# Batch 0 of a routed attention kernel: transposes of pairs 4 to 6 placed up to three steps sooner, alpha's column moved from step 39 to step 10

## Chip, cores and metric

The kernel runs on one core of one Trainium2 chip. The metric is the device time of one execution in microseconds (us), lower is better. A profile is one execution taken by the hardware profiler; its span is about 1.8 us shorter than the timed value of the same execution. All timed runs quoted as ratios are fast (granted TensorE clock 0.99 to 1.00); of the kernel before, one run of 320.57 us at a clock of 0.95 was left out as slow.

## The reference, cut to what matters

Four batches, eight heads, 768 positions, head size 64. Each query and key is assigned to the nearest of 16 centroids, and a query attends only to keys of its own cluster. The result goes through a hidden layer of 2048 columns with a "snake" activation.

```python
mask = q_assign[:, :, :, None] == k_assign[:, :, None, :]
scores = np.where(mask, scale * (q @ k.T), -1e9);  attn = softmax(scores)
x = (attn @ v) reshaped to [3072, 512]
h = x @ w_in;  g = h + sin(alpha * h)**2 / (alpha + 1e-9);  out = g @ w_out
```

## The kernel before

Heads are done in pairs. Batch 0 is a loop of 48 steps, 12 for each of its pairs 0 to 3. In step i TensorE makes scores for one block of keys, ScalarE takes their exp, and TensorE multiplies an earlier step's exps with V ("PV"). In between TensorE prepares later pairs: it transposes q and k ("T units", four to a pair, three 128x128 transposes each) into one of three PSUM banks, VectorE evicts them (copies them out, so that the bank is free again), and GpSimd casts the result. For each pair VectorE also makes a one-hot of the cluster ("one-hot chain": `asT`, `amax`, the is_equal `ohd`, `ohT`). `at(i, f)` only fixes the place of f in each engine's program order; nothing waits for a clock.

```python
banks = [M1, M2, M0]                       # taken in turn by bank()
def prep_T(m, g, bk=None, eng="dve"):      # one T unit
    ...
    for jj in range(NJ2):                  # 3 transposes on TensorE
        nc.tensor.transpose(out=bk[:, P*jj : P*jj+P], in_=src[:, h, P*jj : P*jj+P], identity=ident_f)
    nc.vector.tensor_scalar_mul(out=s["T32"][:, g, :], in0=bk[:, 0:HS], scalar1=1.0 / QDIV)   # the line shown as L150
def pair_steps(m, make, asn, cast):
    for g, i in make:      at(i, lambda g=g: prep_T(m, g))
    for h in range(2):     at(cast[h], lambda h=h: prep_cast(m, h))        # GpSimd
    ...
    at(asn,     lambda: (prep_asn(m), prep_hot(m, 0)))                    # asT
    at(asn + 1, lambda: (prep_hot(m, 1), prep_hot(m, 2)))                 # amax, is_equal
    at(asn + 2, lambda: (prep_hot(m, 3), prep_move(m)))                   # ohT and its DMA
def pv(i):
    ...                                    # 6 matmuls into OB
    if kt == NJ - 1:                       # last step of a head: free OB
        nc.vector.reciprocal(out=rec, in_=o3[:, :, D : D + 1])
        nc.vector.tensor_tensor(out=s["xs"][:, :, h, :], in0=o3[:, :, 0:D], in1=rec..., op=ALU.mult)
def alpha():
    bk = bank()
    nc.tensor.transpose(out=bk[:, 0:NF], in_=a_sb, identity=ident_f[0:NF, 0:NF])
    nc.vector.tensor_copy(out=alpha_col, in_=bk[:, 0:NF])                    # L639
    nc.vector.tensor_scalar_add(out=ralpha, in0=alpha_col, scalar1=1e-9)     # L640
    nc.vector.reciprocal(out=ralpha, in_=ralpha)                             # L641
...
for r in range(ASTEPS):                    # 48 steps
    scores(i); expo(i)
    ahead = b == 0 and r % NJ == 1         # in these steps the plan stands before PV
    if ahead: (plan of step i)
    for d in due.get(r, []): pv(base + d)
    if not ahead: (plan of step i)
```

The softmax here doesn't subtract the row's maximum and nothing guards it: scores larger than these inputs give would overflow.

Of the kernel before, what the change touches and what calls it, by code (L numbers as in the profile page):

```python
# [22 lines left out]
def kernel(  # L23
# [78 lines left out]
    def bank():  # L102
        while True:
            i = turn[0] % 3
            turn[0] += 1
            if i not in held:
                return banks[i]
# [27 lines left out]
    def prep_T(m, g, bk=None, eng="dve"):  # L135

        s = st[m]
        if "T32" not in s:
            s["T32"] = trp.tile([P, 4, HS], F32, tag="T32", name="T32")
        h, t = divmod(g, 2)  # L140
        src = s["q32" if t == 0 else "k32"]
        bk = bank() if bk is None else bk
        for jj in range(NJ2):
            nc.tensor.transpose(  # L144
                out=bk[:, P * jj : P * jj + P],
                in_=src[:, h, P * jj : P * jj + P],
                identity=ident_f,
            )
        if eng == "dve":
            nc.vector.tensor_scalar_mul(  # L150
                out=s["T32"][:, g, :], in0=bk[:, 0:HS], scalar1=1.0 / QDIV
            )
        else:
            nc.scalar.activation(
                out=s["T32"][:, g, :], in_=bk[:, 0:HS], func=ACTF.Copy, scale=1.0 / QDIV
            )
# [203 lines left out]
    def x_T(m, bk=None):  # L360
        b, hp = pair_of[m]
        xs = st[m]["xs"]
        xt_ps = (bank() if bk is None else bk).bitcast(BF16)[:, 0:S]
        for j in range(NJ):
            nc.tensor.transpose(
                out=xt_ps.rearrange("c (i j a) -> c j i a", i=4, j=NJ)[:, j],
                in_=xs[:, j, :, :],
                identity=ident_b,
            )
        nc.vector.tensor_copy(out=xT[:, hp, :], in_=xt_ps)  # L370
        st[m].clear()
# [3 lines left out]
    def x_D(m):  # L375
        hp = pair_of[m][1]
        if hp == 0:
            xq[0] = xqp.tile([P, 2 * S], BF16, tag="xq", name="xq")
        nc.vector.transpose(  # L379
            out=xq[0][:, S * hp : S * hp + S],  # L380
            in_=st[m]["xs"].rearrange("p j h (e d) -> p (h e) j d", e=2),
        )
        st[m].clear()
# [178 lines left out]
    def at(i, fn):  # L562
        plan.setdefault(i, []).append(fn)
# [10 lines left out]
    def pair_steps(m, make, asn, cast):  # L574
        for g, i in make:
            at(i, lambda g=g: prep_T(m, g))
        for h in range(2):
            at(cast[h], lambda h=h: prep_cast(m, h))
        if asn is None:
            return  # L580
        at(asn, lambda: (prep_asn(m), prep_hot(m, 0)))
        at(asn + 1, lambda: (prep_hot(m, 1), prep_hot(m, 2)))
        at(asn + 2, lambda: (prep_hot(m, 3), prep_move(m)))
# [9 lines left out]
    for m, make, asn, cast in (  # L593
        (1, (), 1, (0, 0)),
        (2, ((0, 4), (2, 5), (1, 6), (3, 7)), 8, (7, 8)),
        (3, ((0, 12), (1, 14), (2, 16), (3, 17)), 20, (14, 18)),
        (4, ((0, 19), (1, 23), (2, 24), (3, 26)), 32, (24, 28)),
        (5, ((0, 28), (1, 30), (2, 31), (3, 34)), 38, (31, 35)),
        (6, ((0, 35), (1, 36), (2, 37), (3, 40)), None, (37, 41)),
    ):  # L600
        pair_steps(m, make, asn, cast)
    for g, i in enumerate((41, 42, 43)):
        at(i, lambda g=g: prep_T(NHP + 3, g))
    for h in range(2):
        at(ASTEPS + 4 + 2 * h, lambda h=h: prep_cast(NHP + 3, h))
# [5 lines left out]
    for b in range(1, B):  # L611
        for n in range(NHP):
            m = NHP * b + 3 + n
# [10 lines left out]
    for m in range(NP):  # L624
        if m % NHP != NHP - 1:
            if m < NHP:
                at((18, 29, 44)[m], lambda m=m: x_T(m))
            elif m % NHP == 2:
                at(STEPS * (m + 1) + 4, lambda m=m: x_T(m))
            else:  # L630
                at(STEPS * (m + 1) + 5, lambda m=m: x_D(m))
# [8 lines left out]
        nc.vector.tensor_scalar_add(out=ralpha, in0=alpha_col, scalar1=1e-9)  # L640
        nc.vector.reciprocal(out=ralpha, in_=ralpha)  # L641

    at(39, alpha)
    def load_w_in(n):
        nc.gpsimd.dma_start(
            out=w_in_bf[:, :, 512 * n : 512 * n + 512],
            in_=moe_w_in[:, 512 * n : 512 * n + 512].rearrange("(kk p) f -> p kk f", p=P),
        )
# [24 lines left out]
    for b in range(B):  # L673
        base = ASTEPS * b
        fill = Fill(b - 1) if b else None
        for r in range(ASTEPS):
            i = base + r
# [105 lines left out]
```

## Time and profile before

| kernel before | |
|---|---|
| time, median of the first 3 runs | 313.48 us (312.94 to 313.51) |
| span of the profiled execution | 312.8 us |
| TensorE busy | 302.7 us |
| batch 0's exps: first starts, last ends | 11.91 us, 53.75 us |

From the page of the kernel before: its span, the busy time of the engines (PE is TensorE, PEld its weight loads, DVE is VectorE, ACT ScalarE, POOL GpSimd), and the shares of the chain that ended last.

```profile
span 312.8 us, 7228 instructions
...
PE 302.7 (97%) x2750; PEld 179.9 (58%) x2750; DVE 208.9 (67%) x367; ACT 239.5 (77%) x324; POOL 139.0 (44%) x222
...
PE 86%; DVE 5%; ACT 4%; DMA 2%; issue 1%; SPq 1%; ACTq 0%; DVEq 0%
```

TensorE is the bounding engine over the whole span. A busy share of 97% says where to look, not how much is left: the Trainium skill, "Perfetto Trace Analysis", section "Identifying the Most-Contended Engine", warns that matmul busy time is no good measure of the distance to the limit, because matmuls are pipelined. So the useful question is where TensorE waits. Busy time by stretches (microseconds from the span's start, then busy time of each engine with its instruction count) shows one such place at the end of batch 0's loop.

```profile
core 0: us, PE busy (x) PEld busy (x) DVE busy (x) ACT busy (x) POOL busy (x), PEclk, DMA share, GB/s
36.00:48.00 12.00, 12.00 (x157) 8.51 (x154) 10.82 (x22) 10.57 (x14) 11.32 (x14) 1.00 1.06 243
48.00:53.30 5.30, 4.10 (x59) 2.87 (x57) 3.55 (x9) 4.05 (x6) 3.68 (x5) 1.00 0.59 101
```

In the second stretch TensorE is busy for 4.10 of 5.30 us. VectorE's order of work before and in that stretch (start, duration, engine, line, operation, result and sources) tells why.

```profile
44.69 0.58 DVE L243 STREAM_TRANSPOSE asT<-M 128x384 f32<-128x384 f32 x1
45.31 0.55 DVE L246 TENSOR_REDUCE amax<-asT 128x24 f32<-128x384 f32 x1
45.90 1.10 DVE L254 TENSOR_TENSOR ohd<-asT,amax 128x384 bf16<-128x384 f32 x1
46.92 0.16 DVE L639 COPY alpha_col<-M 128x16 f32<-128x16 f32 x1
47.12 0.60 DVE L640 TENSOR_SCALAR ralpha<-alpha_col 128x16 f32<-128x16 f32 x1
47.75 0.25 DVE L641 RECIPROCAL ralpha<-ralpha 128x16 f32<-128x16 f32 x1
48.13 0.58 DVE L280 STREAM_TRANSPOSE ohT<-ohd 128x384 bf16<-128x384 bf16 x1
48.63 1.91 DVE L150 TENSOR_SCALAR T<-M 128x384 f32<-128x384 f32 x4
50.46 0.18 DVE L352 RECIPROCAL rec<-OB 128x6 f32<-128x6 f32 x1
50.68 0.56 DVE L353 TENSOR_TENSOR xs<-OB,rec 128x384 bf16<-128x384 f32 x1
```

The is_equal (L254) of pair 5 takes 1.10 us. Alpha's three operations follow (L639 to L641), and the add of 16 columns alone takes 0.60 us. Only then comes the one-hot's transpose at 48.13, and four evictions (L150) stand behind it, then rec and xs. GpSimd was casting meanwhile.

```profile
45.77 1.92 POOL L186 CAST QK<-T 64x768 bf16<-64x768 f32 x2
```

Casts occupy GpSimd from 45.77 to 47.69. TensorE's own timeline shows what it waited for (in brackets: idle time just before, and who ended it).

```profile
49.20 0.55 PE L144 MATMUL M<-ident_f,q 128*128 128x128 f32 x3 [0.57 <-DVE T L150]
...
51.29 0.52 PE L341 MATMUL OB<-VX,pT 128*128 128x65 bf16 x12 [0.36 <-DVE xs L353]
```

Step 43's transposes had to wait for a bank (the weight load that goes with them had stood for 0.96 us), and PV of step 45 had to wait for xs. The chain of waits in the same stretch (start, duration, what) runs through VectorE without a break.

```profile
48.64 1.90 DVE T L150 x4
50.54 0.11 DVE rec L352
...
50.68 0.57 DVE xs L353
```

### The profile page before, as it was taken

Reading aid. Unit: us, or ns where it says so; the run is one execution under the profiler, and the core shown is the slowest. Engines: PE = TensorE matmul, PEld = TensorE weight load, DVE = VectorE, ACT = ScalarE, POOL = GpSimd, SP = SyncE. Lnnn points to the kernel's source line nnn. Section 1 sums busy time; section 2 is a strip of 40 time slices with the busy share of each in tenths; the row PEclk is TensorE's granted clock in tenths of the full one; section 3 lists DMA queues with packets and bytes.
Section 4 is the critical chain, followed back from the end, with each engine's and each line's share of the span. In section 5 each row is a group of like instructions: output and inputs, shape, how many; then the busy total and the mean of one; then the engine's idle time right before and its main releaser. Section 6 shows DMA issues by size and latency. Waiting matters only on the chain.

```text
span 312.8 us, 7228 instructions
## 1 busy us (share of the span) xinstructions
PE 302.7 (97%) x2750; PEld 179.9 (58%) x2750; DVE 208.9 (67%) x367; ACT 239.5 (77%) x324; POOL 139.0 (44%) x222
## 2 busy tenths in 40 slices
PE   8899998999999999999999999999999999999994
PEld 3466776455456656555556556555556666555443
DVE  4777796688866876677867877686935313687711
ACT  6589988787679998688679998688679999777200
POOL 5979997109506099985006079980001190000000
PEclk9999999999999999999999999999999999999999
DMA  7549996958753567991044477420011121000032
GB/s 232 146 159 292 310 232 128 196 93 285 233 135 79 106 163 171 261 347 60 0 124 113 98 171 163 114 84 2 0 67 49 37 49 39 34 0 2 0 134 69
DMA packets 28674, 38.92 MB, mean 124 GB/s; under 512 B 5072, under 2 KB 22496, under 8 KB 28640
## 3 DMA queue, kind: packets, MB, share of 16 engines
q0 software_dynamic: 10240, 21.11, 25.8%
q1 hardware_dynamic: 18160, 17.30, 20.6%
q8 instruction: 22, 0.36, 0.5%
q14 instruction: 12, 0.10, 0.1%
q10 hardware_dynamic: 240, 0.06, 0.1%
HBM read 27.30 MB, written 6.29 MB: 107 GB/s over the span
## 4 chain that ended last, share of the span: by engine, by line
PE 86%; DVE 5%; ACT 4%; DMA 2%; issue 1%; SPq 1%; ACTq 0%; DVEq 0%
PE M L394 19%; PE S L425 17%; PE S L326 12%; PE OB L341 10%; PE M L425 8%; PE S L327 6%; PE OB L394 5%; PE M L214 3%; DMA QK<-ohT 2%; PE S L394 2%; ACT pT L332 2%; PE M L144 2%; DVE gT L450 2%; ACT s_sb L438 1%; DVE T L150 1%; DVE u_sb L446 1%
## 5 line engine op out<-in xcount | busy, mean ns | idle before, releaser
L332 ACT ACTIVATE pT<-S 128x768 bf16<-128x768 f32 x192 | 143.7, 810 | 17.6 <-PE S L327 16.1
L394 PE MATMUL M<-w_out_bf,gT 128*128 128x512 bf16 (+1 forms) x288 | 90.7, 373 | 0.2
L326 PE MATMUL S<-QK 80*128 80x512 bf16 x192 | 72.9, 380 | 1.5 <-DMA QK<-ohT 1.2
L425 PEld LDWEIGHTS <-w_in_bf 128*128 128x128 bf16 x512 | 49.3, 98 | 37.9 <-issue 1.8
L341 PEld LDWEIGHTS <-pT 128*128 128x128 bf16 x1152 | 56.1, 97 | 21.4 <-issue 0.5
L425 PE MATMUL S<-xT,w_in_bf 128*128 128x512 bf16 x352 | 65.0, 326 | 0.7 <-DVE gT L450 0.6
L341 PE MATMUL OB<-VX,pT 128*128 128x65 bf16 x1152 | 61.3, 193 | 0.6 <-DVE xs L353 0.4
L438 ACT ACTIVATE s_sb<-S,alpha_col 128x768 bf16<-128x768 f32 (+2 forms) x45 | 39.3, 885 | 23.7 <-PE S L425 16.1
L394 PEld LDWEIGHTS <-gT 128*128 128x128 bf16 x400 | 39.0, 97 | 30.7 <-issue 5.4
L327 PE MATMUL S<-QK 80*128 80x256 bf16 x192 | 51.9, 270 | 0.0
L191 POOL TENSOR_SCALAR QK<-T 64x384 bf16<-64x384 f32 x64 | 34.9, 546 | 37.9 <-DMA T<-Tq 33.8
L450 DVE SCALAR_TENSOR_TENSOR gT<-u_sb,ralpha,S 128x768 bf16<-128x768 bf16 (+2 forms) x45 | 44.7, 996 | 9.7 <-ACT u_sb L443 6.8
L387 POOL DMA_DIRECT2D xT<-xq x48 | 25.8, 544 | 29.0 <-DVE xq L379 28.0
L186 POOL CAST QK<-T 64x768 bf16<-64x768 f32 x32 | 27.1, 848 | 7.7 <-DVE T L150 3.5
L425 PE MATMUL M<-xT,w_in_bf 128*128 128x512 bf16 (+1 forms) x160 | 29.9, 326 | 0.0
L352 DVE RECIPROCAL rec<-OB 128x6 f32<-128x6 f32 x32 | 6.2, 193 | 34.8 <-PE OB L341 34.8
L446 DVE TENSOR_TENSOR u_sb<-s_sb 128x768 bf16<-128x768 bf16 (+2 forms) x41 | 23.7, 580 | 7.0 <-ACT s_sb L438 7.0
L327 PEld LDWEIGHTS <-QK 80*128 80x128 bf16 x192 | 18.8, 98 | 16.1 <-issue 2.0
L203 POOL CAST VX<-v 128x768 bf16<-128x768 f32 x16 | 13.7, 859 | 28.7 <-issue 27.8
L438 ACT ACTIVATE s_sb<-M,alpha_col 128x512 bf16<-128x512 f32 (+1 forms) x40 | 20.9, 573 | 7.2 <-PE M L425 7.2
L450 DVE SCALAR_TENSOR_TENSOR gT<-u_sb,ralpha,M 128x512 bf16<-128x512 bf16 (+1 forms) x40 | 22.8, 611 | 5.4 <-ACT u_sb L443 5.0
L394 PE MATMUL OB<-w_out_bf,gT 128*128 128x512 bf16 (+1 forms) x80 | 26.2, 358 | 0.1
(83 smaller groups left out, 282.2 us busy)
## 6 DMA issues: line engine op xcount, KB each, us to landing
T<-Tq SPq DMA_DIRECT2D x64, 96.0 KB, 2.5
out_dram<-o_sb SPq DMA_DIRECT2D x23, 256.0 KB, 2.1
v<-in_v_dram POOLq DMA_DIRECT2D x14, 384.0 KB, 4.6
q<-in_q_dram POOLq DMA_DIRECT2D x13, 384.0 KB, 6.4
k<-in_k_dram POOLq DMA_DIRECT2D x13, 384.0 KB, 6.8
w_in_bf<-in_moe_w_in_dram POOLq DMA_DIRECT2D x4, 512.0 KB, 7.9
w_out_bf<-in_moe_w_out_dram POOLq DMA_DIRECT2D x4, 512.0 KB, 9.1
xT<-xq POOLq DMA_DIRECT2D x48, 24.0 KB, 2.2
```

The source lines that it names most:

```text
L186: nc.gpsimd.tensor_copy(out=QK[0:D, m % NQK, h, :, HS * par : HS * par + HS], in_=src)
L191: nc.gpsimd.tensor_scalar(out=QK[0:D, m % NQK, h, t].rearrange("c (n i a) -> c i n a", i=4, a=32)[:, 2 * par : 2 * par + 2], in0=src[:, t] ...
L326: nc.tensor.matmul(out=dst[:, 0:512], lhsT=lhsT, rhs=T[:, 0, 0:512], start=True, stop=True)
L327: nc.tensor.matmul(out=dst[:, 512:S], lhsT=lhsT, rhs=T[:, 0, 512:S], start=True, stop=True)
L332: nc.scalar.activation(out=pT, in_=area(i)[:, 0:S], func=ACTF.Exp, scale=escale)
L341: nc.tensor.matmul(out=o3[:, j, :], lhsT=pT[:, P * j : P * j + P], rhs=VX[m % NVX][:, h, jof(m // NHP, kt), :], start=(kt == 0 and j == 0) ...
L387: nc.gpsimd.dma_start(out=xT[32 * g : 32 * g + 32, 0:2, QS * i : QS * i + QS], in_=xq[0].rearrange("p (h g n) -> p h g n", h=2, g=4)[32 * ...
L394: nc.tensor.matmul(out=bk[:, lo:hi], lhsT=gT[:, f, P * mt : P * mt + P], rhs=w_out_bf[:, f, lo:hi], start=(f == 0), stop=(f == NF - 1),)
L425: nc.tensor.matmul(out=ar[lo // 512][:, 0 : hi - lo] if isinstance(ar, tuple) else ar[:, lo:hi], lhsT=lhsT, rhs=xT[:, kk, :].rearrange("c ...
L438: nc.scalar.activation(out=s_sb[:, lo:hi], in_=src, func=ACTF.Sin, scale=alpha_col[:, f : f + 1])
L446: nc.vector.tensor_tensor(out=u_sb[:, lo:hi], in0=s_sb[:, lo:hi], in1=s_sb[:, lo:hi], op=ALU.mult)
L450: nc.vector.scalar_tensor_tensor(out=gT[:, f, lo:hi], in0=u_sb[:, lo:hi], scalar=ralpha[:, f : f + 1], in1=src, op0=ALU.mult, op1=ALU.add,)
```

## The change

The intent was to take work out of VectorE's queue near the end of the loop: eleven of the twelve T units of pairs 4 to 6 come one to three steps sooner, and alpha, which is not needed before the hidden layer, goes to step 10. Three smaller moves go with it: the casts of pairs 4 to 6 come one or two steps sooner, pair 7's third T unit one step later, and pair 2's x transposes one step sooner.

```diff
-        (4, ((0, 19), (1, 23), (2, 24), (3, 26)), 32, (24, 28)),
-        (5, ((0, 28), (1, 30), (2, 31), (3, 34)), 38, (31, 35)),
-        (6, ((0, 35), (1, 36), (2, 37), (3, 40)), None, (37, 41)),
+        (4, ((0, 19), (1, 22), (2, 23), (3, 24)), 32, (23, 26)),
+        (5, ((0, 26), (1, 28), (2, 30), (3, 31)), 38, (30, 34)),
+        (6, ((0, 34), (1, 35), (2, 36), (3, 37)), None, (36, 40)),
     ...
-    for g, i in enumerate((41, 42, 43)):
+    for g, i in enumerate((41, 42, 44)):        # T units of pair 7
     ...
-                at((18, 29, 44)[m], lambda m=m: x_T(m))
+                at((18, 29, 43)[m], lambda m=m: x_T(m))
     ...
-    at(39, alpha)
+    at(10, alpha)
```

## The prediction

> **What bounds the kernel now.** TensorE: the page's engine table has it busy 302.7 of 312.8 us, and the chain that ended last is 86% TensorE. The change touches only the attention loop of batch 0 (48 steps of scores, exp and PV, about 11.4 to 53.8 us). There TensorE's queue is full, 12.00 busy of 12.00 us in the stretch 36 to 48 us, but only 4.10 of 5.30 us in 48.0 to 53.3 us (busy time by stretches). That hole is the target. The chain of waits puts VectorE on the path there: four T evictions, 48.64 to 50.54, then rec and xs to 51.25.
>
> How it arises (timeline): VectorE runs pair 5's one-hot chain from 44.69; the is_equal takes 1.10 us instead of 0.56, alpha's three operations take 46.92 to 48.00 (the add of 16 columns 0.60), and the one-hot's transpose comes only at 48.13. Four T evictions queue behind. So TensorE's transposes of step 43 wait 0.96 us for a PSUM bank (scores of step 43 start at 48.14, of step 44 at 49.77), and PV of step 45 waits about 0.5 us for xs (to 51.29).
> The two slow operations end as the GpSimd casts of 45.77 to 47.69 end. The Trainium skill, "SBUF — State Buffer", section "Who interferes with whom", says that VectorE operations with two SBUF inputs, or in two-port modes, and GpSimd exclude each other on one port pair; 1.10 against 0.56 agrees.
>
> **What changes.** No work is added or removed. Pair 4's transposes come one or two steps sooner, pairs 5 and 6 one to three, and alpha (TensorE about 0.16 us, VectorE 1.0) goes from step 39 to step 10. At step 10 TensorE waits for the one-hot DMA of step 12 anyway (idle 0.38 us in 20 to 22 us), and VectorE's next eviction starts only at 22.72, after 0.60 us of idleness; without a cast beside it alpha should take about 0.5 us. a_sb landed by 10 us.
>
> **Costing.** A step with one transpose unit takes 0.87 us (TensorE bound), one without about 0.72 (exps 0.72 apart, ScalarE bound).
> - Before step 38 one more unit is done: +0.15 to +0.35 us. GpSimd is full from 19.5 to 47.7 (13.7 of 14.0 us in 22 to 36), so its casts hardly come sooner.
> - Steps 39 and 40 lose alpha and a unit: 0.95 and 0.88 become about 0.70 and 0.76: -0.4.
> - Steps 43 to 46 lose the wait for the bank (1.63 becomes 0.85) and part of the wait for xs, perhaps 0.3 us of which stays: -0.9 in sum.
> Together the loop ends about 1.0 us sooner (0.7 to 1.4). Behind it comes the hidden layer, whose TensorE queue is nearly full to the end; its weights land before use, and batch 1's loads are paced by it. So nearly all should reach the end.
>
> **Predicted**: 312.4 us, range 311.7 to 313.2; faster by over 2%: 0.01, within 2%: 0.98, slower by over 2%: 0.01.
>
> **What would show it.** Right: no wait of transposes for T evictions in steps 41 to 44; the add under alpha well below 0.6 us; last exp of batch 0 ending about 1 us sooner (53.75 before); idle TensorE there down from 1.2 to about 0.4 us; later stages unchanged in length. The is_equal of pair 5 may stay near 1.1 us.
> Wrong: a new TensorE gap at steps 12 to 15 or 22 to 27 (VectorE now crowded by the one-hots of pairs 2 and 3), or the gain given back after 56 us.
>
> **What would make it wrong.** The one-hot chain meeting casts at other places, so that evictions pile up again; the extra unit before step 38 costing its full 0.36 us or waiting for banks; weight DMAs displaced; or run to run spread (0.6 us over three runs), which is more than half the effect.

## The result

The changed kernel took 312.38 us (median of 4 runs, 311.55 to 312.81), beside 313.26 us for the kernel before (4 runs). The ratio is 0.9969, with a 95% interval of 0.9945 to 0.9993. A ratio here is the mean time of one kernel's fast runs over that of the other's in the same rounds, so it is not quite the ratio of the medians. Two later sets of five rounds gave 0.9965 (0.9949 to 0.9981) and 0.9955 (0.9925 to 0.9985). All lie below 1.

The page after, same parts as before:

```profile
span 310.5 us, 7224 instructions
...
PE 302.7 (97%) x2750; PEld 180.0 (58%) x2750; DVE 208.6 (67%) x367; ACT 239.7 (77%) x324; POOL 139.3 (45%) x222
...
PE 87%; ACT 5%; DVE 4%; DMA 2%; issue 1%; SPq 0%; ACTq 0%; DVEq 0%
```

Busy time of every engine is unchanged, as it must be when work is only moved. The span is 2.3 us shorter, but that is not all due to the change: the last matmul ends at 307.18 us instead of 308.18, and the rest is the landing of the last store, which took 4.6 us after the last matmul in this profile of before, 4.8 us in one later profile of the changed kernel, and 3.3 us in all others, before's second one included. The stretches after:

```profile
36.00:48.00 12.00, 11.91 (x157) 8.37 (x156) 10.67 (x21) 10.74 (x15) 11.59 (x16) 1.00 1.01 238
48.00:53.30 5.30, 4.86 (x69) 3.58 (x68) 2.58 (x6) 5.02 (x7) 4.90 (x7) 1.00 0.96 167
```

TensorE's idle time in 48.0 to 53.3 us fell from 1.20 to 0.44 us. VectorE's order after:

```profile
45.07 0.58 DVE L243 STREAM_TRANSPOSE asT<-M 128x384 f32<-128x384 f32 x1
...
46.28 1.07 DVE L254 TENSOR_TENSOR ohd<-asT,amax 128x384 bf16<-128x384 f32 x1
47.39 0.58 DVE L280 STREAM_TRANSPOSE ohT<-ohd 128x384 bf16<-128x384 bf16 x1
47.89 1.01 DVE L150 TENSOR_SCALAR T<-M 128x384 f32<-128x384 f32 x2
49.00 0.56 DVE L370 COPY xT<-M 128x768 bf16<-128x768 bf16 x1
49.48 0.18 DVE L352 RECIPROCAL rec<-OB 128x6 f32<-128x6 f32 x1
49.70 0.56 DVE L353 TENSOR_TENSOR xs<-OB,rec 128x384 bf16<-128x384 f32 x1
```

Alpha is gone from it; two evictions (pair 7's first two) and the copy of pair 2's x transposes (L370, which had stood behind xs), not four evictions, stand before rec and xs; and ohT, at 47.39, comes 0.74 us sooner. The is_equal still takes 1.07 us. TensorE's timeline after:

```profile
49.31 0.49 PE L144 MATMUL M<-ident_f,q 128*128 128x128 f32 x3
...
50.30 0.52 PE L341 MATMUL OB<-VX,pT 128*128 128x65 bf16 x12 [0.17 <-DVE xs L353]
```

The transposes of pair 7's third unit, which had waited for a bank, no longer wait, and the wait for xs fell from 0.36 to 0.17 us. Alpha in its new place, step 10, on VectorE:

```profile
22.22 0.14 DVE L639 COPY alpha_col<-M 128x16 f32<-128x16 f32 x1
22.39 0.17 DVE L640 TENSOR_SCALAR ralpha<-alpha_col 128x16 f32<-128x16 f32 x1
22.60 0.25 DVE L641 RECIPROCAL ralpha<-ralpha 128x16 f32<-128x16 f32 x1
22.98 0.56 DVE L150 TENSOR_SCALAR T<-M 128x384 f32<-128x384 f32 x1
```

There it takes 0.63 us from the first start to the end of the last operation, and the add takes 0.17 us.

By intervals between the starts of exps, so that the varying start of the loop drops out (both columns from the traces):

| stretch | before | after | difference |
|---|---|---|---|
| exp 12 to exp 22 (behind alpha's new place) | 8.36 | 8.36 | 0.00 |
| exp 22 to exp 38 (one T unit more) | 13.41 | 13.53 | +0.12 |
| exp 38 to exp 43 (alpha and a unit fewer) | 4.79 | 4.40 | -0.39 |
| exp 43 to the end of exp 47 (the waits) | 5.02 | 4.04 | -0.98 |
| sum | 31.59 | 30.34 | -1.25 |

(The sum adds unrounded terms.) The loop starts 0.18 us later in the second trace and ends 0.98 us sooner; the last exp of batches 1, 2 and 3 ends 0.99, 0.98 and 1.01 us sooner. Nothing was given back.

### The profile page after: what moved, and what is told of

The parts are those of the page before. It is cut to its first block, busy times and chain, and to the rows that moved or that the text cites. A ratio compares the mean times of both kernels' runs of the same rounds, so it can differ in the third digit from the quotient of the medians.

```text
span 310.5 us, 7224 instructions
## 1 busy us (share of the span) xinstructions
PE 302.7 (97%) x2750; PEld 180.0 (58%) x2750; DVE 208.6 (67%) x367; ACT 239.7 (77%) x324; POOL 139.3 (45%) x222
## 4 chain that ended last, share of the span: by engine, by line
PE 87%; ACT 5%; DVE 4%; DMA 2%; issue 1%; SPq 0%; ACTq 0%; DVEq 0%
PE M L394 19%; PE S L425 17%; PE S L326 13%; PE OB L341 10%; PE M L425 8%; PE S L327 6%; PE OB L394 5%; PE M L214 3%; ACT pT L332 3%; PE S L394 2%; DMA QK<-ohT 2%; PE M L144 2%; DVE gT L450 2%; ACT s_sb L438 1%; DVE u_sb L446 1%; PE S L501 1%
```

## The experiments

The measure in what follows is the time from the start of exp 12 to the end of exp 47 of batch 0, read from each trace. It repeats to 0.01 us for the changed kernel (30.34, 30.34, 30.35), while whole times scatter by 0.6 us or more, so whole times cannot rank these variants. The theories:

- **A**: VectorE's queue behind pair 5's one-hot chain is what binds; anything that shortens it helps, whatever it is.
- **B**: the T units carry the gain and alpha's move is incidental.
- **C and D**: the slow is_equal and add are waits for a port that GpSimd's casts hold (C), so that the size of the loss depends on when GpSimd happens to run (D).
- **E**: alpha's TensorE transpose and bank cost the time, not VectorE's time.

### 1. Alpha alone (alpha_only)

```diff
 (kernel before)
-    at(39, alpha)
+    at(10, alpha)
```

> The kernel before with alpha alone moved from step 39 to step 10; all units stay. Theory A (what counts is how long VectorE's queue is behind pair 5's one-hot chain): the one-hot's transpose comes about 1.1 us sooner (47.0 instead of 48.13), the evictions behind it too, TensorE's wait of 0.96 us in step 43 falls under 0.2 us, and from the first to the last exp of batch 0 it takes 40.7 to 41.0 us (41.84 before, 40.67 after the change): alpha's move carries most of the gain. Theory B (the units' earlier steps carry it, alpha is small): 41.6 to 41.8 us, the wait stays over 0.6 us.

Measured: 30.33 us from exp 12, what the whole change reaches; first to last exp 40.48 us, 0.22 below A's range and far from B's. TensorE's wait for a bank is gone. The ratio was 0.9974 (0.9959 to 0.9990). Alpha alone was enough in this trace. But is_equal took 0.56 us in it, so the variant had luck with GpSimd (see 5).

### 2. The units alone (units_only)

```diff
 (changed kernel)
-    at(10, alpha)
+    at(39, alpha)
```

> The changed kernel with alpha left in step 39: units alone. Theory A: alpha is back in VectorE's queue (about 1.2 us with the wait for the cast), so evictions and xs of steps 41 to 45 come about 0.9 us later than with the whole change; TensorE waits for xs in step 45 for about 1 us instead of 0.17; first to last exp 41.4 to 41.8 us, so nearly no gain over 41.84. Theory B: 40.7 to 41.0 us, nearly the whole gain.

Measured: 30.78 us from exp 12; first to last exp 41.01 us, well outside A's range and at the edge of B's. The units alone give 0.81 of the 1.25 us, and alpha alone gives all of it. So B, by which alpha is incidental, falls by experiment 1. The miss of A has a visible reason: in this trace alpha's add took 0.17 us, not 0.60. With the slow add the same queue would have been 0.43 us longer, which gives about 41.4 us (an estimate), the lower end of A's range. So these two traces don't show how the gain is divided; see under the table for that. The ratio was 0.9980 (0.9962 to 0.9998).

### 3. The changed kernel again (after_again, after_third)

> The changed kernel once more, beside the others on the same chip: ratio to before 0.9965 (0.995 to 0.998); first to last exp of batch 0 40.67 us within 0.1; end of the last matmul 1.0 us sooner than before. The page's span may again differ by more than that through the landing of the last store.

> The changed kernel beside spread, on the same chip: ratio to before 0.9967 (0.995 to 0.998), exp 12 to exp 47 30.34 us within 0.1, whatever GpSimd's phase.

Measured: 30.34 and 30.35 us from exp 12; the last matmul ended 1.66 and 1.06 us sooner than in before's first profile, of which the loop's own start differs by 0.28 us sooner and 0.26 us later. First to last exp took 40.49 us in after_again, 0.08 outside the range given, because the first twelve steps took 10.15 instead of 10.33 us. is_equal took 1.06 and 1.21 us in these traces without any effect on the stretch: the changed order has slack for it.

### 4. The kernel before again (before_again)

> The kernel before, unchanged, for a second profile. Theory A (VectorE's queue, the order of the program): from the start of exp 12 of batch 0 to the end of exp 47 it takes 31.6 us again within 0.1 (30.3 with the change, twice). Theory D (the phase between GpSimd's casts and VectorE's operations, which depends on when the v load lands, is a large part): is_equal of pair 5 and alpha's add may take 0.56 and 0.17 us this time, and the stretch then comes out up to 0.9 us shorter.

Measured: 30.87 us, where the first profile of the same program had 31.59. VectorE in this second profile:

```profile
46.28 0.81 DVE L254 TENSOR_TENSOR ohd<-asT,amax 128x384 bf16<-128x384 f32 x1
...
47.21 0.17 DVE L640 TENSOR_SCALAR ralpha<-alpha_col 128x16 f32<-128x16 f32 x1
...
47.79 0.58 DVE L280 STREAM_TRANSPOSE ohT<-ohd 128x384 bf16<-128x384 bf16 x1
```

is_equal took 0.81 instead of 1.10 us and the add 0.17 instead of 0.60; together 0.72 us, which is exactly by how much ohT starts sooner after exp 38 and by how much the stretch is shorter. A's "31.6 within 0.1" falls; D holds. The first profile, from which the prediction was read, holds a wait that not every execution has. Which of the two is the commoner is not known: this run took 312.85 us, at the fast end of its set (the same kernel took 312.82 to 315.35 us there, median 313.82), and the ratios of the whole change, 0.9955 to 0.9969, amount to 1.0 to 1.4 us, nearer to the gain over the first profile (1.25) than to that over the second (0.53).

### 5. GpSimd's casts moved (casts_later, casts_away)

```diff
 casts_later (kernel before)
-        (6, (...), None, (37, 41)),
+        (6, (...), None, (44, 45)),
-        (ASTEPS - 1, load_w_out, 1), (ASTEPS - 1, load_w_in, 3), (ASTEPS - 1, load_w_out, 2), (ASTEPS - 1, load_w_out, 3),
+        (38, load_w_out, 1), (38, load_w_in, 3), (38, load_w_out, 2), (38, load_w_out, 3),
 casts_away: the loads in step 35 instead of 38, and also
-        (5, (...), 38, (31, 35)),
+        (5, (...), 38, (31, 43)),
```

> The kernel before, VectorE's and TensorE's order untouched, alpha in step 39; only GpSimd's order: the four weight loads of step 47 are issued in step 38, and the casts of pair 6 come after them (steps 44 and 45). Theory C (the crowding is mostly waiting for the port that GpSimd's casts hold): pair 5's is_equal falls from 1.10 to about 0.56 us, alpha's add from 0.60 to about 0.17, the evictions come about 0.9 us sooner, the wait of 0.96 us in step 43 nearly goes, and first to last exp takes 40.8 to 41.1 us. If the slow operations have another cause they stay at 1.1 and 0.6 us and nothing moves (41.8 us).

Measured: 31.11 us; first to last exp 41.26 us, between the two ranges given; ratio 0.9977 (0.9962 to 0.9992). is_equal fell to 0.63, but the add stayed at 0.60. GpSimd's timeline of casts_later shows that the experiment had not removed what it meant to: a load of v landed late, and pair 5's own cast came late and ran to 47.40, just when the add ended.

```profile
43.24 0.83 POOL L203 CAST VX<-v 128x768 bf16<-128x768 f32 x1 [2.13 <-DMA v<-in_v_dram]
...
45.45 1.95 POOL L186 CAST QK<-T 64x768 bf16<-64x768 f32 x2
```

So casts_away moves that cast too. By then the runs suggested a law:

> The kernel before, alpha in step 39 and all units where they were; GpSimd issues the weight loads of step 47 in step 35 and does the casts of pair 5's second half and of pair 6 behind them, so that no cast runs beside pair 5's one-hot chain. The runs so far with before's units lie on one line: exp 12 to exp 47 takes 27.40 us plus the start of pair 5's one-hot transpose after exp 38 (4.19 gives 31.59, 3.47 gives 30.87, 3.71 gives 31.11), down to a floor of 30.33. Theory D plus A: is_equal takes 0.56 us, alpha's add 0.17, the transpose starts 3.2 us after exp 38, and the stretch takes 30.6 us (30.5 to 30.75), without a unit or alpha moved. If the slow operations do not come from the casts, the transpose starts at 3.5 or later and the stretch takes 30.9 us or more.

Measured: 30.62 us. The transpose started 3.22 us after exp 38; 27.40 + 3.22 = 30.62. VectorE in casts_away:

```profile
45.52 0.56 DVE L254 TENSOR_TENSOR ohd<-asT,amax 128x384 bf16<-128x384 f32 x1
...
46.20 0.17 DVE L640 TENSOR_SCALAR ralpha<-alpha_col 128x16 f32<-128x16 f32 x1
...
46.78 0.58 DVE L280 STREAM_TRANSPOSE ohT<-ohd 128x384 bf16<-128x384 bf16 x1
```

GpSimd beside it issues loads and casts only afterwards:

```profile
44.63 1.51 POOL L651 DMA_DIRECT2D w_out_bf<-in_moe_w_out_dram  x2
46.09 0.79 POOL L645 DMA_DIRECT2D w_in_bf<-in_moe_w_in_dram  x1
46.83 1.75 POOL L186 CAST QK<-T 64x768 bf16<-64x768 f32 x2
```

With no unit and no alpha moved, and not one instruction changed on VectorE or TensorE, the order of GpSimd's program alone recovered 0.97 us against before's first profile and 0.25 us against its second. C and D hold. is_equal (45.52 to 46.08) and the add (46.20 to 46.37) ran beside the issue of DMAs and were not slowed by it.

The traces kept of all 14 executions of this document settle it further. They hold 70 is_equals of batch 0. The 29 that started with no cast running took 0.56 us. One started 0.14 us before a running cast's end and took 0.56 us as well. The other 40 started with 0.20 us or more of a cast still to go, and each ended 0.41 or 0.42 us after that cast's end, however long that made it (0.63 to 1.21 us). The two adds of 0.60 us ended 0.03 us after a cast's end. It works the other way round too: four casts that started up to 0.25 us after an is_equal took 1.00 to 1.19 us instead of about 0.82, while that is_equal took 0.56. So the one that starts first holds up the other. That what they share is a port is not shown by the traces.

### 6. Alpha later instead of sooner (alpha_late), and its time put back as other work (reduce_twice_more)

```diff
 alpha_late (kernel before)
-    at(39, alpha)
+    at(46, alpha)
 reduce_twice_more: alpha_late, and
+    for _ in range(2):
+        at(39, lambda: prep_hot(5, 1))      # the same max reduce again, same values
```

> The kernel before with alpha in step 46 instead of 39 (not sooner, but later, behind the evictions, where VectorE is idle for 2.6 us). Theory A: all that counts is that alpha leaves the queue of steps 39 to 45; exp 12 to exp 47 takes 30.2 to 30.6 us, as with alpha in step 10 (30.3). If step 10 itself is special (its bank, its early place), it stays over 31 us.

> The kernel before with alpha in step 46, and in step 39 two more runs of pair 5's max reduce (same values, 0.55 us each on VectorE, no TensorE work). Result right. Theory A: VectorE's queue is as long again as before, about 1.15 us more; the T evictions come 1.1 us later, TensorE waits for a bank in step 43 again (0.5 to 1.0 us) and for xs (0.3 to 0.5 us): exp 12 to exp 47 takes 31.2 to 31.7 us. Rival E (what cost time was alpha's TensorE transpose and its bank, not VectorE's time): 30.2 to 30.6 us as in alpha_late.

Measured: alpha_late 30.40 us, so step 10 is not special: step 46, on the other side of the crowded queue, does as well to 0.07 us. reduce_twice_more 30.82 us, which is below the range that A gave and above E's. The two reduces took 0.92 us up to the next operation, not the 1.15 expected, and the one-hot transpose started 0.81 us later than in alpha_late (3.36 against 2.55); that is a delay of 0.81 us, of which 0.42 appeared in the stretch, because the first part only used up slack. Pure VectorE time, with no TensorE work, brings the loss back: E is not the main cause. A small part of E shows in one interval: with alpha in step 39 it takes 2.17 us from exp 38 to exp 40, without it 1.92.

### What these runs say together

| kernel | alpha in step | T units | is_equal | alpha's add | ohT starts after exp 38 | exp 12 to exp 47 |
|---|---|---|---|---|---|---|
| before | 39 | old | 1.10 | 0.60 | 4.19 | 31.59 |
| casts_later | 39 | old | 0.63 | 0.60 | 3.71 | 31.11 |
| before_again | 39 | old | 0.81 | 0.17 | 3.47 | 30.87 |
| casts_away | 39 | old | 0.56 | 0.17 | 3.22 | 30.62 |
| reduce_twice_more | 46 | old | 0.56 | 0.17 | 3.36 | 30.82 |
| alpha_late | 46 | old | 0.56 | 0.17 | 2.55 | 30.40 |
| alpha_only | 10 | old | 0.56 | | 2.55 | 30.33 |
| units_only | 39 | new | 1.06 | 0.17 | 3.72 | 30.78 |
| after | 10 | new | 1.07 | 0.17 | 3.07 | 30.34 |
| after_again | 10 | new | 1.06 | | 3.05 | 30.34 |
| after_third | 10 | new | 1.21 | | 3.21 | 30.35 |

(An empty field was not read off.) With the old units and alpha in step 39, the stretch is 27.40 us plus the start of ohT, to 0.01 us, in four executions of three programs; reduce_twice_more, with alpha elsewhere, lies on the same line if the 0.07 us is added that alpha in step 46 costs in alpha_late. The stretch stops falling at a floor of 30.33 to 30.40 us. What sets the floor was not tested; the changed kernel's chain of waits from 36 us on runs through TensorE, with one exp of 0.82 us, up to 48.98 us, and then through 1.2 us of VectorE's work to PV of step 45; and spread (see 7), which deals TensorE's work out otherwise, gets to 30.03. So one microsecond of VectorE delay costs one microsecond above the floor and nothing below it. units_only lies 0.33 us lower than casts_later at the same start of ohT (3.72 and 3.71): from the start of ohT to the end of xs it takes 2.64 instead of 3.11 us, with three operations between ohT and rec instead of four, and the unit that was moved costs 0.13 us before exp 38. The whole change sits on the floor with room: it stays there with an is_equal of 1.21 us.

A comparison of single traces mixes the change with GpSimd's phase, so the gain has to be divided at equal phase. At an equal start of ohT the units are worth 0.33 us, as just said. Alpha alone with an is_equal of 1.10 us would have its ohT at 3.09, and by the line take about 30.5 us (an estimate), so in the phase of before's first profile alpha's move is worth about 1.1 us; with the casts away it is worth 0.29 (30.62 less 30.33). The two remedies thus add until the floor is reached (1.1 and 0.33 are more than the 1.25 measured); where the phase is kind, alpha alone reaches it.

### 7. Attempts at a kernel that beats both (both, spread, spread2)

Three versions were built on the changed kernel. (Lines are numbered anew in them: an eviction is L613, a single transpose L607, the hidden matmuls L429, the write of gT L456.)

```diff
 both: x transposes of pair 2 later; first snake by pieces; hidden column block 3 by pieces
-                at((18, 29, 43)[m], lambda m=m: x_T(m))
+                at((18, 29, 45)[m], lambda m=m: x_T(m))
+            (snake(0): square and gT of columns 0:512, then of 512:768)
+            (hidden_mm(3): all four k for columns 0:512, then all four for 512:768)
 spread: single transposes instead of units of three
+    for m, share in ((3, {12: 2, 13: 2, 14: 3, 15: 1, 16: 2, 17: 2}), ... (7, {43: 2, 45: 2, 46: 2, 47: 3})):
+        (so many single transposes of pair m in each step; the eviction after every third;
+         pair 1's x transposes in two halves, in steps 28 and 29, pair 2's in step 44;
          the casts of pairs 4 to 6 one to four steps later)
 spread2: the same dealt out otherwise, behind the one-hot operations of each step; casts as in casts_away
```

> The changed kernel with two more changes of order, meant to beat both. (1) pair 2's x transposes in step 45 instead of 43, so that VectorE does xs of step 43 first: TensorE's wait for xs of 0.17 us in step 45 goes, exp 12 to exp 47 takes 30.1 to 30.2 us instead of 30.34. (2) Batch 0's first snake squares and finishes its first 512 columns before the other 256, and hidden column block 3 does all its matmuls of the first 512 columns before those of the rest, so that it waits for the first part of gT only: TensorE's wait of 0.61 us there falls to 0.0 to 0.3 us. Together 0.4 to 0.8 us, ratio to before 0.9945 (0.993 to 0.9965). If the dependence is on the whole of the PSUM area, (2) brings nothing or loses 0.1 us.

Measured: 0.9964 (0.9932 to 0.9997), the stretch 30.28 us. The ratio lies just inside the range given, but that is no success: the change without these additions reached 0.9955 to 0.9969. The first part worked as far as it went: the wait for xs is gone, but it was worth 0.06 us only. The second part made things worse. TensorE's wait before hidden column block 3, after the change:

```profile
58.76 1.46 PE L425 MATMUL S<-xT,w_in_bf 128*128 128x512 bf16 x8 [0.61 <-DVE gT L450]
```

and in this version:

```profile
59.49 1.46 PE L429 MATMUL S<-xT,w_in_bf 128*128 128x512 bf16 x8 [0.91 <-DVE gT L456]
```

The first matmul of the block waits for the finish of all of gT (the program has one wait there and none later), so finishing the first part early helps nothing, and the second part now ends later: 0.91 us of waiting instead of 0.61.

> Meant to beat both: the changed kernel with the transposes of pairs 3 to 7 dealt out singly, about two in every step from 12 on, instead of three in some steps and none in others; pair 1's x transposes in two halves, pair 2's in step 44. Steps with three transposes took 0.87 us (TensorE bound) and steps with none 0.72 (ScalarE bound, TensorE with about 0.2 us to spare); with two in each both engines need about 0.75. Expected: exp 12 to exp 47 takes 29.0 to 29.8 us instead of 30.34, ratio to before 0.994 (0.9925 to 0.996). If VectorE's evictions or the rotation of three banks now bind (a unit holds its bank for two steps), TensorE shows waits for T evictions and the stretch stays at 30 us or more.

Measured: 0.9973 (0.9933 to 1.0012), the stretch 30.03 us. Most steps did come down to 0.76 us. What took the gain back is seen on VectorE,

```profile
29.15 0.58 DVE L243 STREAM_TRANSPOSE asT<-M 128x384 f32<-128x384 f32 x1 [0.35 <-PE M L214]
30.54 0.56 DVE L613 TENSOR_SCALAR T<-M 128x384 f32<-128x384 f32 x1 [0.81 <-PE S L327]
31.02 0.54 DVE L246 TENSOR_REDUCE amax<-asT 128x24 f32<-128x384 f32 x1
```

where an eviction in step 21 stood ahead of `amax` and waited 0.81 us for TensorE, so that the whole chain of pair 3 slid, and in step 27 TensorE waited for xs:

```profile
34.43 0.54 PE L341 MATMUL OB<-VX,pT 128*128 128x65 bf16 x12 [0.34 <-DVE xs L353]
```

> The last try for a kernel that beats both. In spread, steps took 0.76 us as meant, but the stretch lost 0.5 us in step 28, where TensorE waited for xs: an eviction of pair 4 stood ahead of pair 3's one-hot chain in VectorE's queue in step 21 and held it up by 1.3 us. Here the single transposes stand behind the one-hot operations in each step, no unit is finished in the step in which a head's last PV is done (so xs goes first), three transposes fill TensorE's wait for the last exps in step 47, and the casts and weight loads stand as in casts_away. Expected: exp 12 to exp 47 takes 29.1 to 29.7 us (30.34 with the change, 30.03 in spread), no TensorE wait for xs over 0.2 us in it; ratio to before 0.9935 (0.9915 to 0.9955). If it stays at 30 us, TensorE's and ScalarE's cadence binds, not VectorE's order.

Measured: 0.9970 (0.9931 to 1.0009), the stretch 30.42 us, worse than spread. Now TensorE waits for evictions, 0.5 us in one place (step 35, by the trace), in the list of waits of TensorE from 22 to 53 us (who, for whom, us in total, times, longest):

```profile
PE M L607 <- DVE T L613: 0.5, 1, 0.5
```

None of the three is shown to be faster than the change; all their intervals overlap with it. All three gave right results. The expectation that cadence would bind if it stayed at 30 us was not borne out: in the longest steps of both spread versions (27 in spread, 35 in spread2) TensorE again waits for VectorE. No run tests this apart. Whether a good order would reach the 29.1 to 29.7 us expected is open. So is how often each phase of GpSimd occurs: the timed runs have no traces.

## Why the prediction was right

- **What bounds.** Right. The hole of 1.2 us fell to 0.44 us, as said (about 0.4). It holds most of the gain (0.98 of the 1.25 us); the rest is 0.39 us between exp 38 and exp 43, less 0.12 us before.
- **How the hole arises.** Right, and now tested: the table above shows VectorE's queue in it, and casts_away shows the casts' part. What the Trainium skill says in "SBUF — State Buffer", section "Who interferes with whom" (that a VectorE operation with two SBUF inputs, or in a two-port mode, and a GpSimd one that reads SBUF exclude each other), agrees: with the casts away, is_equal took 0.56 and the add 0.17 us, beside them up to 1.21 and 0.60.
- **Alpha in step 10.** Right: it took 0.63 us there (about 0.5 expected), and exp 12 to exp 22 took 8.36 us before and after.
- **One more unit before step 38.** The cost was 0.12 us, just under the 0.15 to 0.35 stated.
- **Steps 39 and 40.** -0.39 us over exp 38 to exp 43, with -0.4 predicted.
- **Steps 43 to 46.** -0.98 us with -0.9 predicted, and 0.17 us of the wait for xs stayed (0.3 predicted).
- **Passed on to the end.** Right: the last matmul ended 1.01 us sooner. 312.38 us was measured and 312.4 predicted. That the loop's end, 0.98 us sooner, met the "about 1.0" so closely is partly luck: the stretch gained 1.25 us, and a loop that started 0.18 us later and first twelve steps that took 0.08 us more hid the rest.
- **What the prediction did not see.** It took the profile of before as the program's fixed behaviour. A second profile of the same program is 0.72 us better in this stretch, so by the traces the gain is 1.25 us against one execution, inside the 0.7 to 1.4 stated, and 0.53 us against another, outside it; that the forecast held rests in part on this phase. It named the danger that casts meet the chain at other places, but not that this already varies from run to run. It also did not say how the gain divides between alpha and the units.

## What to carry to other kernels

Where an engine's queue bounded the stretch, shortening it paid one for one down to a floor and then nothing; two remedies for the same queue add only down to that floor, so try the cheapest alone first (here one line that moves alpha). Before costing a change from one profile, look for operations of unusual length beside another engine's work and take a second profile: the excess may be the phase of that execution. Where whole times scatter more than the effect, compare a stretch between two instructions that every variant has.

## What the Trainium skill lacked or had wrong

- "SBUF — State Buffer", section "Who interferes with whom": its rule that the order of issue decides who blocks agrees with the runs (a cast that was running held is_equal up to 1.21 us; an is_equal that had started stretched a cast to 1.00 us or more), but it doesn't say what that does to measurements: the same program gave 1.10 and 0.81 us for one is_equal, 0.60 and 0.17 us for one add of 16 columns, and 30.87 and 31.59 us for the stretch, in two executions.
- The same section says, marked as inferred, that an operation with two inputs in SBUF does not collide with descriptor generation. Experiment 5 agrees: is_equal took 0.56 us wholly beside GpSimd's DMA issues. The add, a `tensor_scalar`, took its shortest time of 0.17 us beside such an issue as well.
- "TensorE: Matmul & The Clock Gate", part "PE-mode transpose", gives some 275 ns for a 128x128 bf16 transpose. Here a float32 one shows 270 to 332 ns in the records of batch 0's loop, but three of them add only about 0.36 us to the chain, 0.12 us each, since they overlap; for planning steps the second number is the one that counts.
